# 32 x 32 block transposes on VectorE with transfers in place of TensorE transposes, in four of eight batches, and a later preparation of MLP2's first weights

## The chip, the cores and the metric

The program runs on one core of a Trainium2 chip. The metric is the device time of one execution in microseconds (us), as a median over runs. TensorE (PE in the profile) multiplies matrices, VectorE (DVE), ScalarE (ACT) and GpSimd (POOL) work elementwise, and SyncE (SP) issues nearly all DMA transfers, in order, on one queue.

## The reference

Eight batches go through a cross attention between 512 tokens and 32 state rows per head (8 heads of 64), a first MLP with a softmax-like gate and a normalisation, and a second MLP. Cut to what matters:

```python
# attention, per batch and head: x is 512 x 64, state is 32 x 64
a     = softmax(scale * x @ state.T);  xread = a @ state
a2    = softmax(scale * state @ x.T);  sread = a2 @ x
x = concat(xread, sread)                     # 8 batches of 544 rows of 512
# MLP1 (w_in 512 x 1024, w_out 1024 x 512)
h = x @ w_in
solu = h * softmax(h)
ln = (solu - mean) / sqrt(var + 1e-6) * g_ln
x = ln @ w_out
# MLP2 (w_in 512 x 2048, w_out 2048 x 512)
h = x @ w_in
out = (h * sigmoid(1.702 * h)) @ w_out
```

## The kernel before

Every product of MLP1 and MLP2 is computed from a high and a low part of each factor: three matmuls (high by high, low by high, high by low) for one product, so each factor must first be split in two by ScalarE and VectorE or GpSimd.

The work is described as steps (an engine or a choice of engines, an estimated cost, tiles that are read and written, and a due time), and a planner (`Plan`) puts all steps of the program in one order before the program is built. Each engine then runs its steps strictly in that order. Due times such as 205 are in the planner's own time, which is not the time of the trace. Tiles lie in numbered slots of SBUF: `NSLOT` slots of 2 KB per partition for most tiles (kind "s"), `NRAW` slots for weights as they come from memory (kind "r"), `NWIDE` for the 1024 columns wide tiles of MLP1 (kind "d"). When the last tile of kind "d" is done, that memory becomes further "s" slots for MLP2 (`pl.more`).

The batches overlap. While batch b is in MLP1's first product (`mlp1`, four tiles of 128 tokens, whose product needs two PSUM banks each), batch b-1 is in the second (`mlp1_out`, eight blocks k of 128 inner columns), and batch b+1 is in attention. In `attention`, `x_T(j)` transposes the x of two heads: TensorE makes four 128 x 128 transposes into a PSUM bank, and ScalarE or VectorE copies the bank out. In MLP1, `z_T(b, k)` does the same with the four normalised tiles u of a batch: four 128 x 128 transposes on TensorE, then ScalarE multiplies by g and writes the high part (`zhi`), and VectorE writes the low part (`zlo`), both from PSUM. `mlp1_out(b, k)` then needs both parts. `store_x2` copies the finished batch out of PSUM and stores it (`scr`).

MLP2's weights are 64-bit floats in memory. `to_f32` turns a block of them into 32-bit ones (two passes of ScalarE, three of VectorE, one of GpSimd). MLP2 multiplies in a form with seven instead of eight block products, so the blocks are also added to one another (`sums`, four passes of VectorE) and split. `prepare_up(k, q)` does this for a quarter of the first weight matrix (four blocks, seven results) and stores the results in DRAM (`kept3`); `load_up(j)` reads a part j of four back before the products of step (batch, j) start. Parts j = 0, 1 come from the quarters with q = 0, parts j = 2, 3 from those with q = 1. MLP2 runs over steps in the order (0,0), (1,0), (0,1), (1,1), (0,2), ... of seven products each (`up`), and later over the second weight matrix (`down`).

Of the kernel before, what the change touches and what calls it, by code (L numbers as in the profile page):

```python
# [8 lines left out]
F32 = mybir.dt.float32  # L9
F32R = mybir.dt.float32r  # L10
# [4 lines left out]
AF = mybir.ActivationFunctionType  # L15
ALU = mybir.AluOpType
AX = mybir.AxisListType

NSLOT = 79
NWIDE = 7  # L20
NRAW = 2
AHEAD = 30.092
KF = 11.222
LOOK = 27.436
# [8 lines left out]
LEAD = 62.849  # L33
KEEP = 5
PP = 1.33
FIRST = "d"


class Tl:
# [301 lines left out]
def attention_solu_gelu(ctx: ExitStack, tc: tile.TileContext, x, state, w1, w2, g_ln, w3, w4, out):  # L341
# [28 lines left out]
    pl.kind("s", slot_p, NSLOT)  # L370
    pl.kind("d", first_p, NWIDE)
    pl.kind("r", slot_p, NRAW)
    pl.first, pl.late = first_p, None
    pl.kind("t", slot_p, 4)
    pl.kind("y", slot_p, 28)
# [8 lines left out]
    def ACT(c):  # L384
        return [("act", c)]

    def DVE(c):
        return [("dve", c)]
# [7 lines left out]
    def DMA(c=0.55):  # L396
        return [("dma", c)]
# [102 lines left out]
    def attention(b):  # L500
# [14 lines left out]
        for j in range(1, NP):  # L515
            load_x(b, j)

        def x_T(j):
            p = tl("m", [P, 512], F32, f"pxT{b}_{j}")
            xt[j] = tl("s", [P, S], F32, f"xT{b}_{j}")  # L520

            def go(e):
                for c in range(C):
                    e.transpose(p()[:, c * P:(c + 1) * P], xn[b, j]()[:, c].rearrange("p a d -> p (a d)"), ident)

            do(PE(.44), go, [xn[b, j]], [p], key())
            do([("act", .48), ("dve", .6)], lambda e: copy(e, xt[j](), p()), [p], [xt[j]])
# [199 lines left out]
    def mlp1(b, i, key):  # L727
# [21 lines left out]
        def hf():  # L749
# [17 lines left out]
        do([("dve", .72), ("pool", 1.2)], lambda e: e.tensor_scalar(u(), u(), s()[:, 3:4], s()[:, 7:8], op0=ALU.add, op1=ALU.mult),  # L767
           [s, u], [u])
        return mm

    def z_T(b, k, key):
        n = n_tiles[b] * P
# [71 lines left out]
    def prepare_up(k, q, due):  # L844

        blocks = [to_f32(rows(w3, k + 2 * j, q + 2 * i), f"w3_{k}{q}{i}{j}", due - 3, keep=KEEP)
                  for i in range(2) for j in range(2)]
        for i, t in enumerate(sums("a", blocks, f"w3_{k}{q}")):
            for h, t in zip("hl", split(t, f"w3s{i}_{k}{q}", due)):
                o = kept3[i, q, h]  # L850
                do(DMA(), lambda e, o=o, t=t: e.dma_start(out=o()[:, k], in_=t().bitcast(F32)), [t], [o], key=due + 5,
                   nbytes=P * 2048, join=began3.get((i, q, h)))
                began3.setdefault((i, q, h), pl.steps[-1])

    def load_up(j, due, after):

        q, c = divmod(j, 2)
        for i in range(7):
            w = W3[i, j] = [tl("s", [P, 2, 256], F32R, f"w3r{i}_{j}{h}") for h in "hl"]
            for h, t in zip("hl", w):  # L860
                o = kept3[i, q, h]
                do(DMA(), lambda e, o=o, t=t, c=c: e.dma_start(out=t().bitcast(F32), in_=o()[:, :, 256 * c:256 * c + 256]),
                   [o], [t], key=due, after=after, keep=RK, nbytes=P * 2048)
# [254 lines left out]
             for i in range(7) for q in range(2) for h in "hl"}  # L1118
    began3 = {}
    for n, (q, k) in enumerate((q, k) for q in range(2) for k in range(2)):  # L1120
        prepare_up(k, q, SLOT + (n + 1) * (base2 - 40 - SLOT) / 4)
    attention(0)
    for b in range(B):
        if b + 1 == DIRECT:
# [14 lines left out]
    for b in range(B + 1):  # L1139
        acc = [tl("w", [P, 2, 512], F32, f"accA{b}_{a}") for a in range(2)]  # L1140
        base = (b + 1) * SLOT if b < B else B * SLOT + 27
        per = SLOT / K1 if b < B - 1 else (3.3 if b < B else 1.7)
        if b == 0:
            base, per = M2A, M2S
        for k in range(K1):
            z_T(b, k, base + k * per - ZL)
            mlp1_out(b, k, acc, base + k * per)
        store_x2(b, acc, base + K1 * per + 2)
    per = 7 * PP
# [4 lines left out]
        at[c, j] = base  # L1154
        base += per if c < B else 4 * PP
    base3 = base + 3 * PP
    for j in range(NM // 2):
        load_up(j, at[0, j] - 6, [last[B]])
    x2, kept4 = {}, {}
    for n, (c, j) in enumerate(steps):  # L1160
# [17 lines left out]
            base += per  # L1178
        finish(c, acc, base)
    down_plain(base)  # L1180
    pl.more(2 * NWIDE)
    pl.plan()
    pl.emit()

# [25 lines left out]
```

## Time and profile before

| | |
|---|---|
| median of 3 runs | 1157.05 us (1156.01 to 1157.98) |
| the profiled execution | 1153.79 us, of which the span of instructions is 1152.0 us |
| TensorE busy | 1103.9 us, 96% of the span |
| VectorE busy | 798.0 us, 69% |
| ScalarE, GpSimd busy | 643.4 us, 254.9 us |
| mean granted TensorE clock | 0.988 |

Busy times overlap between engines. TensorE's matmuls are pipelined and their recorded durations overlap one another, so a matmul's price is the distance from one start to the next. An engine's idle time only costs something where the work that ends last waits for it; a share of the whole span hides stretches in which another engine is the full one.

### The profile page before, as it was taken

Reading aid. Unit: us, or ns where it says so; the run is one execution under the profiler, and the core shown is the slowest. Engines: PE = TensorE matmul, PEld = TensorE weight load, DVE = VectorE, ACT = ScalarE, POOL = GpSimd, SP = SyncE. Lnnn points to the kernel's source line nnn. Section 1 sums busy time; section 2 is a strip of 40 time slices with the busy share of each in tenths; the row PEclk is TensorE's granted clock in tenths of the full one; section 3 lists DMA queues with packets and bytes.
Section 4 is the critical chain, followed back from the end, with each engine's and each line's share of the span. In section 5 each row is a group of like instructions: output and inputs, shape, how many; then the busy total and the mean of one; then the engine's idle time right before and its main releaser. Section 6 shows DMA issues by size and latency. Waiting matters only on the chain.

```text
span 1152.0 us, 21763 instructions
## 1 busy us (share of the span) xinstructions
PE 1103.9 (96%) x8239; PEld 1000.0 (87%) x8239; DVE 798.0 (69%) x1336; ACT 643.4 (56%) x1187; POOL 254.9 (22%) x218
## 2 busy tenths in 40 slices
PE   5889889989999989999999999999999999999998
PEld 2567667767777868999999999999999999999998
DVE  6999895695886754427567656715578897788780
ACT  6687765975785645447566656645344443344440
POOL 3865582553575430001011001000000000000000
PEclk8899999999999999999999999999999999999999
DMA  8214253063140449757677576649963254344411
GB/s 244 58 55 129 72 171 110 26 205 105 37 183 2 155 165 344 267 184 266 220 247 251 207 241 208 229 147 397 379 212 94 91 164 141 104 142 147 166 59 52
DMA packets 148600, 192.27 MB, mean 167 GB/s; under 512 B 44304, under 2 KB 90384, under 8 KB 148496
## 3 DMA queue, kind: packets, MB, share of 16 engines
q1 hardware_dynamic: 148400, 190.76, 49.9%
q8 instruction: 64, 1.05, 0.4%
q14 instruction: 40, 0.33, 0.1%
q10 hardware_dynamic: 96, 0.13, 0.0%
HBM read 108.01 MB, written 82.84 MB: 166 GB/s over the span
## 4 chain that ended last, share of the span: by engine, by line
PE 77%; DVE 16%; ACT 3%; issue 2%; DMA 1%; POOL 0%; SPq 0%; DVEq 0%; ACTq 0%; POOLq 0%
PE psum L961 9%; PE psum L960 9%; PE psum L962 9%; PE psum L1039 9%; PE psum L1040 9%; PE psum L1041 9%; PE psum L418 5%; PE psum L420 5%; PE psum L419 5%; DVE w_w L445 2%; DVE w_w L440 2%; DVE u L756 2%; DVE w_w L443 1%; ACT v L459 1%; DVE zlo L785 1%
## 5 line engine op out<-in xcount | busy, mean ns | idle before, releaser
L1039 PE MATMUL psum<-w4r,hi_g 128*128 128x256 f32 x896 | 251.6, 281 | 1.6 <-DVE oc L1050 1.6
L1040 PE MATMUL psum<-w4r,hi_g 128*128 128x256 f32 x896 | 251.5, 281 | 0.0
L1041 PE MATMUL psum<-w4r,lo_g 128*128 128x256 f32 x896 | 251.5, 281 | 0.0
L1039 PEld LDWEIGHTS psum<-w4r,hi_g 128*128 128x128 f32 x896 | 169.1, 189 | 1.8 <-ACT hi_g L459 1.8
L1041 PEld LDWEIGHTS psum<-w4r,lo_g 128*128 128x128 f32 x896 | 169.0, 189 | 0.0
L1040 PEld LDWEIGHTS psum<-w4r,hi_g 128*128 128x128 f32 x896 | 168.9, 189 | 0.0
L459 ACT CAST hi_g<-a_g 128x512 fp32r<-128x512 f32 x124 | 75.1, 620 | 120.6 <-DVE a_g L830 86.3
L447 POOL TENSOR_TENSOR w_w<-w_w,raw_w 128x512 uint32<-128x512 uint32 x48 | 66.6, 1395 | 290.3 <-DVE w_w L445 209.5
L972 DVE TENSOR_TENSOR c<-psum,u 128x512 f32<-128x512 f32 x64 | 44.1, 690 | 107.8 <-PE psum L962 68.8
L418 PE MATMUL psum<-zhi,hi_w 128*128 128x512 f32 (+1 forms) x288 | 115.9, 402 | 1.7 <-DVE u L756 1.1
L419 PE MATMUL psum<-zlo,hi_w 128*128 128x512 f32 (+1 forms) x288 | 110.3, 383 | 0.1
L420 PE MATMUL psum<-zhi,lo_w 128*128 128x512 f32 (+1 forms) x288 | 110.2, 383 | 0.0
L907 DVE TENSOR_TENSOR lo_g<-a_g,hi_g 128x512 fp32r<-128x512 f32 x128 | 83.8, 685 | 18.9 <-PE psum L1040 7.3
L944 ACT ACTIVATE t<-c 128x512 f32<-128x512 f32 x96 | 60.6, 632 | 47.8 <-DVE c L972 47.2
L907 DVE TENSOR_TENSOR lo_g<-gr,hi_g 128x512 fp32r<-128x512 f32 x104 | 70.9, 685 | 10.7 <-ACT hi_g L459 9.2
L459 ACT CAST hi_g<-gr 128x512 fp32r<-128x512 f32 x104 | 61.4, 618 | 28.1 <-PE psum L1040 15.3
L783 ACT ACTIVATE zhi<-psum,g_sb 128x512 fp32r<-128x512 f32 (+1 forms) x72 | 46.9, 664 | 41.7 <-PE psum L777 34.8
L418 PEld LDWEIGHTS psum<-zhi,hi_w 128*128 128x128 f32 x288 | 54.5, 189 | 15.1 <-issue 4.1
L785 DVE SCALAR_TENSOR_TENSOR zlo<-psum,g_sb,zhi 128x512 fp32r<-128x512 f32 (+1 forms) x72 | 51.0, 715 | 22.1 <-ACT zhi L783 20.8
L420 PEld LDWEIGHTS psum<-zhi,lo_w 128*128 128x128 f32 x288 | 54.4, 189 | 11.4
L961 PE MATMUL psum<-lo_x,w3r_3h 128*128 128x256 f32 x224 | 63.0, 281 | 0.0
L962 PE MATMUL psum<-hi_x,w3r_3l 128*128 128x256 f32 x224 | 63.0, 281 | 0.0
(249 smaller groups left out, 3134.9 us busy)
## 6 DMA issues: line engine op xcount, KB each, us to landing
g<-t SPq DMA_DIRECT2D x136, 256.0 KB, 2.3
gr<-g SPq DMA_DIRECT2D x136, 256.0 KB, 3.7
w4r<-w4k SPq DMA_DIRECT2D x56, 256.0 KB, 5.2
raw_w<-in_moe_w_in SPq DMA_DIRECT2D x24, 512.0 KB, 4.8
raw_w<-in_moe_w_out SPq DMA_DIRECT2D x24, 512.0 KB, 4.9
xb<-scr SPq DMA_DIRECT2D x34, 256.0 KB, 6.0
scr<-x SPq DMA_DIRECT2D x16, 512.0 KB, 3.2
out<-oc SPq DMA_DIRECT2D x32, 256.0 KB, 3.1
```

The source lines that it names most:

```text
L418: nc.tensor.matmul(o, lhi, rhi, start=first, stop=False)
L419: nc.tensor.matmul(o, lhi, rlo, start=False, stop=False)
L420: nc.tensor.matmul(o, llo, rhi, start=False, stop=last)
L447: do(POOL(1.23), lambda e: e.tensor_tensor(u(), u(), raw()[:, :, 0], op=ALU.add), [w, raw], [w], key=due)
L459: e.copy(o, i)
L907: do(DVE(.68), lambda e: e.tensor_tensor(flat_(lo), flat_(t), flat_(hi), op=ALU.subtract), [t, hi], [lo], key=due)
L960: nc.tensor.matmul(o, wh()[:, k, cut], hi()[:, k, :], start=first and not mi + k, stop=False, **OPEN)
L961: nc.tensor.matmul(o, wh()[:, k, cut], lo()[:, k, :], start=False, stop=False, **OPEN)
L962: nc.tensor.matmul(o, wl()[:, k, cut], hi()[:, k, :], start=False, stop=bool(mi and k), **OPEN)
L1039: nc.tensor.matmul(o, hi()[:, mi, cut], wt[:, 0], start=first, stop=False, **OPEN)
L1040: nc.tensor.matmul(o, hi()[:, mi, cut], wt[:, 1], start=False, stop=False, **OPEN)
L1041: nc.tensor.matmul(o, lo()[:, mi, cut], wt[:, 0], start=False, stop=2 * j + mi == NM - 1 and u == 1, **OPEN)
```

## The change

Three things change. First, for batches 4 to 7 the x of two heads is no longer transposed by TensorE. Four transfers bring x from memory so that 32 x 32 blocks already lie where they belong, and one VectorE pass transposes each block in place (`x_T_dma`). The untransposed x is still loaded as well. Second, for the same batches `z_T` runs only for k = 0 to 3. The other half is made by `z_turn`: four VectorE passes transpose the 32 x 32 blocks of the four u tiles into a wide tile, sixteen transfers move the blocks from SBUF to SBUF to their places, and then ScalarE and VectorE make the high and the low part for k = 4 to 7, now from SBUF instead of PSUM. Two wide tiles each for the two sides (kind "z", `NZ`) take the place of eight "s" slots. Third, the four calls of `prepare_up` had due times 111.4, 182.4, 253.3 and 324.3 in the planner's time; now three have 205, 255 and 310, and the fourth comes after MLP2's first step has been planned, 16 before step (0,2).

```diff
-NSLOT = 79
+NSLOT = 71
+NZ = 2
+ZB = 4
+XD = 4
-FIRST = "d"
+FIRST = "dz"
...
+        def x_T_dma(j):
+            t = tl("s", [P, C, S // (C * 32), 32], F32, f"xb{b}_{j}")
+            xt[j] = tl("s", [P, S], F32, f"xT{b}_{j}")
+            first = None
+            for q in range(4):
+                src = x[b, 2 * j + q // 2].rearrange("(r t c) d -> t c r d", t=32, c=C)[:, :, :, 32 * (q % 2):32 * (q % 2) + 32]
+                s = do(DMA(.65), lambda e, q=q, src=src: e.dma_start(out=t()[32 * q:32 * q + 32], in_=src), writes=[t],
+                       nbytes=P * 1024, join=first)
+                first = first or s
+            key()
+            do(DVE(.6), lambda e: e.transpose(out=xt[j](), in_=t().rearrange("p c r f -> p (c r f)")), [t], [xt[j]])
+
         def x_T(j):
+            if b >= XD:
+                return x_T_dma(j)
...
+    def z_turn(b, half, due):
+        w = tl("z", [P, C, 512], F32, f"zw{b}_{half}")
+        z = tl("z", [P, C, 512], F32R, f"z{b}_{half}")
+        for i in range(C):
+            t = w.part(lambda ap, i=i: ap[:, i, :])
+            do(DVE(.6), lambda e, t=t, i=i: e.transpose(out=t(), in_=u_t[b, i]()[:, 512 * half:512 * half + 512]),
+               [u_t[b, i]], [t])
...
+        for q0 in range(4):
+            for r in range(4):
+                def go(e, r=r, q=(q0 + r) % 4):
+                    src = w()[32 * r:32 * r + 32].rearrange("f i (k q t) -> f i k q t", q=4, t=32)[:, :, :, q, :]
+                    dst = z()[32 * q:32 * q + 32].rearrange("f i (k r t) -> f i k r t", r=4, t=32)[:, :, :, r, :]
...
+                s = do(DMA(.65), go, [w], [z], key=due - 3, nbytes=P * 1024, join=first)
...
+        for j in range(4):
+            k = 4 * half + j
+            hi = tl("s", [P, C, P], F32R, f"zhi{b}_{k}")
+            lo = z.part(lambda ap, j=j: ap[:, :, j * P:(j + 1) * P])
+            do(ACT(.57), lambda e, hi=hi, lo=lo, k=k: e.activation(hi(), lo().bitcast(F32), AF.Identity,
+                                                                  scale=g_sb[:, k:k + 1]), [lo, g_t], [hi])
+            do(DVE(.67), lambda e, hi=hi, lo=lo, k=k: e.scalar_tensor_tensor(
+                out=lo(), in0=lo().bitcast(F32), scalar=g_sb[:, k:k + 1], in1=hi(), op0=ALU.mult, op1=ALU.subtract),
+               [lo, hi, g_t], [lo])
+            z_t[b, k] = (hi, lo)
...
-        prepare_up(k, q, SLOT + (n + 1) * (base2 - 40 - SLOT) / 4)
+        if n < 3:
+            prepare_up(k, q, (205, 255, 310)[n])
...
+        if ZB <= b < B:
+            z_turn(b, 1, base + 4 * per - ZL)
         for k in range(K1):
-            z_T(b, k, base + k * per - ZL)
+            if (b, k) not in z_t:
+                z_T(b, k, base + k * per - ZL)
...
-    for j in range(NM // 2):
+    for j in range(NM // 4):
+        load_up(j, at[0, j] - 6, [last[B]])
+    prepare_up(1, 1, at[0, 2] - 16)
+    for j in range(NM // 4, NM // 2):
         load_up(j, at[0, j] - 6, [last[B]])
...
-    pl.more(2 * NWIDE)
+    pl.more(2 * NWIDE + 4 * NZ)
```

The planner makes a new order of this. Three places of it follow, in the form "line, operation, written tile <- read tiles, shape"; names begin with the tile's name in the program, with the batch in it.

The first place is VectorE where the second product of batch 3 ends and that of batch 4 begins. `zlo3_7` is the last low part of batch 3, `sml` and `u` are the statistics and tiles of `mlp1`. Before:

```order
L785 SCALAR_TENSOR_TENSOR zlo3_7_2917<-psum_69,g_sb_81,zhi3_7_2908 128x512
L761 TENSOR_SCALAR sml4_3_2869<-sml4_3_2869 128x1
L764 TENSOR_SCALAR sml4_3_2869<-sml4_3_2869 128x1
L752 TENSOR_REDUCE sml5_0_2939<-psum_69 128x1
L756 SCALAR_TENSOR_TENSOR u5_0_2957,sml5_0_2939<-psum_69,u5_0_2957 128x1024
L785 SCALAR_TENSOR_TENSOR zlo4_0_2985<-psum_69,g_sb_81,zhi4_0_2968 128x512
```

The same place now:

```order
L533 STREAM_TRANSPOSE xT6_0_2756<-xb6_0_2654 128x512
L533 STREAM_TRANSPOSE xT6_1_2763<-xb6_1_2685 128x512
L797 STREAM_TRANSPOSE zw4_1_2771<-u4_0_2411 128x512
L775 SCALAR_TENSOR_TENSOR u4_3_2761,sml4_3_2724<-psum_69,u4_3_2761 128x1024
L835 SCALAR_TENSOR_TENSOR zlo3_7_2791<-psum_69,g_sb_81,zhi3_7_2774 128x512
L780 TENSOR_SCALAR sml4_3_2724<-sml4_3_2724 128x1
L880 TENSOR_TENSOR a1_w3_00_2803<-w_w3_0010_2695,w_w3_0011_2706 128x512
L465 CAST hi_w3s4_00_2812<-a1_w3_00_2803 128x512
L797 STREAM_TRANSPOSE zw4_1_2771<-u4_1_2461 128x512
L783 TENSOR_SCALAR sml4_3_2724<-sml4_3_2724 128x1
L797 STREAM_TRANSPOSE zw4_1_2771<-u4_2_2561 128x512
```

Between the same steps of MLP1 there now stand transposes of x and of u, and passes of the first weight preparation (`w3_00`), which stood earlier before.

The second place is SyncE's queue where batch 6 leaves MLP1. `scr6` is the store of batch 6, `w3r` are loads of MLP2's prepared weights. Before:

```order
L807 DMA scr6_101<-x2_6_0_4306 128x1024
L807 DMA scr6_101<-x2_6_1_4323 128x1024
L862 DMA w3r0_0h_4357<-w3k0_0h_104 128x2x256
L862 DMA w3r0_0l_4362<-w3k0_0l_105 128x2x256
L862 DMA w3r1_0h_4367<-w3k1_0h_108 128x2x256
```

The same place now, with all sixteen transfers of batch 7's `z_turn` in one row:

```order
L857 DMA scr6_101<-x2_6_0_4247 128x1024
L806 DMA z7_1_4282<-zw7_1_4043 32x16x32 x16
L857 DMA scr6_101<-x2_6_1_4284 128x1024
L912 DMA w3r0_0h_4371<-w3k0_0h_104 128x2x256
L912 DMA w3r0_0l_4376<-w3k0_0l_105 128x2x256
L912 DMA w3r1_0h_4381<-w3k1_0h_108 128x2x256
```

The sixteen transfers stand behind the first store of batch 6 and ahead of its second store and of all weight loads.

The third place is VectorE in MLP2's first four steps. `c11`, `c12` and `c22` (batch and step behind) are the sums that each step makes of its products. Before, they follow one another:

```order
L972 TENSOR_TENSOR c11_1_0_4970<-psum_69,x1_1_0_4954 128x512
L972 TENSOR_TENSOR c12_0_0_5021<-psum_69,u1_0_0_4885 128x512
L972 TENSOR_TENSOR c22_1_0_5040<-psum_69,u2_1_0_5037 128x512
L972 TENSOR_TENSOR c11_0_1_5071<-psum_69,x1_0_1_5054 128x512
L972 TENSOR_TENSOR c12_1_0_5117<-psum_69,u1_1_0_5005 128x512
```

Now the second half of the fourth preparation (`w3_11`, its last two blocks 1100 and 1101) stands between them:

```order
L1022 TENSOR_TENSOR c12_0_0_4933<-psum_69,u1_0_0_4790 128x512
L444 TENSOR_SCALAR w_w3_1100_4949<-w_w3_1100_4949 128x512
L447 TENSOR_SCALAR w_w3_1100_4949<-w_w3_1100_4949 128x512
L449 SCALAR_TENSOR_TENSOR w_w3_1100_4949<-raw_w3_1100_4831,w_w3_1100_4949 128x512
L1022 TENSOR_TENSOR c22_1_0_4976<-psum_69,u2_1_0_4971 128x512
L444 TENSOR_SCALAR w_w3_1101_4974<-w_w3_1101_4974 128x512
L447 TENSOR_SCALAR w_w3_1101_4974<-w_w3_1101_4974 128x512
L449 SCALAR_TENSOR_TENSOR w_w3_1101_4974<-raw_w3_1101_4854,w_w3_1101_4974 128x512
L880 TENSOR_TENSOR a2_w3_11_5018<-a1_w3_11_4870,w_w3_1100_4949 128x512
L880 TENSOR_TENSOR a3_w3_11_5022<-w_w3_1110_4671,w_w3_1100_4949 128x512
L1022 TENSOR_TENSOR c11_0_1_5040<-psum_69,x1_0_1_4993 128x512
L880 TENSOR_TENSOR a4_w3_11_5049<-w_w3_1101_4974,a2_w3_11_5018 128x512
```

The last sum, `a4`, now stands behind `c11` of step (0,1) in VectorE's order, and step (0,2) needs what is made of it.

## Rows read from the trace of the kernel before

**Rows 1.** The page: busy time, share and instructions of each engine.

```profile
PE 1103.9 (96%) x8239; PEld 1000.0 (87%) x8239; DVE 798.0 (69%) x1336; ACT 643.4 (56%) x1187; POOL 254.9 (22%) x218
```

**Rows 2.** Windows by stage: length, busy PE, PEld, DVE, ACT, POOL, PEclk, DMA.

```profile
130.00:257.00 127.00, 118.22 (x684) 90.02 (x682) 101.88 (x172) 91.80 (x179) 70.00 (x56) 0.99 0.38 122
257.00:403.00 146.00, 142.34 (x860) 111.01 (x859) 107.99 (x193) 97.66 (x194) 73.75 (x66) 1.00 0.29 96
403.00:466.00 63.00, 57.90 (x317) 48.93 (x316) 33.93 (x55) 28.67 (x50) 11.06 (x10) 0.97 0.80 263
466.00:503.00 37.00, 37.00 (x316) 37.00 (x315) 11.13 (x17) 17.47 (x30) 0.00 (x0) 1.00 0.68 235
```

**Rows 3.** Waits of TensorE, 130 to 466: us in total, times, longest.

```profile
PE psum L418 <- DVE u L756: 10.8, 6, 5.1
```

**Rows 4.** Windows where VectorE is full, where it isn't, and behind two waits.

```profile
130.00:170.00 40.00, 36.18 (x234) 27.66 (x232) 39.30 (x65) 28.12 (x60) 29.30 (x23) 0.99 0.47 147
180.00:230.00 50.00, 48.60 (x293) 37.16 (x292) 31.73 (x62) 37.48 (x73) 20.28 (x19) 1.00 0.23 66
340.00:400.00 60.00, 60.00 (x342) 47.99 (x340) 41.67 (x77) 36.09 (x73) 28.14 (x27) 1.00 0.21 75
170.00:180.00 10.00, 9.67 (x44) 7.84 (x45) 4.14 (x8) 5.64 (x9) 3.12 (x4) 0.86 0.15 57
410.00:420.00 10.00, 8.37 (x31) 6.71 (x32) 3.45 (x7) 1.74 (x3) 1.74 (x2) 0.83 0.28 105
```

**Rows 5.** TensorE in order of time around two groups of transposes.

```profile
291.77 0.40 PE L420 MATMUL psum<-zhi,lo_w 128*128 128x512 f32 x1
292.00 0.60 PE L524 MATMUL psum<-ident,xn 128*128 128x128 f32 x4
292.44 0.60 PE L777 MATMUL psum<-ident,u 128*128 128x128 f32 x4
...
293.11 0.39 PE L419 MATMUL psum<-lo_v,ahi 128*128 128x512 f32 x1
```

**Rows 6.** Groups of VectorE by line and shape, 0 to 420: busy, mean ns.

```profile
L785 DVE SCALAR_TENSOR_TENSOR zlo<-psum,g_sb,zhi 128x512 fp32r<-128x512 f32 x56 | 41.1, 743 | 7.3 <-ACT zhi L783 6.2 <-POOL lo_w3s L454 1.0
...
L445 DVE SCALAR_TENSOR_TENSOR w_w<-raw_w,w_w 128x512 uint32<-128x512 uint32 x32 | 28.2, 898 | 0.4
L440 DVE TENSOR_SCALAR w_w<-w_w 128x512 f32<-128x512 f32 x32 | 25.1, 794 | 3.7 <-ACT w_w L439 3.6
L443 DVE TENSOR_SCALAR w_w<-w_w 128x512 uint32<-128x512 uint32 x32 | 20.4, 647 | 0.6
...
L587 DVE STREAM_TRANSPOSE aT<-s 128x512 f32<-128x512 f32 x16 | 11.1, 699 | 2.0 <-POOL s L584 2.0
...
L830 DVE TENSOR_TENSOR a_w<-w_w,w_w 128x512 f32<-128x512 f32 x8 | 10.0, 1250 | 1.0 <-POOL w_w L447 1.0
```

**Rows 7.** VectorE in order of time from 405.91: start, duration.

```profile
405.91 1.79 DVE L830 TENSOR_TENSOR a_w<-w_w,w_w 128x512 f32<-128x512 f32 x1
...
409.74 0.69 DVE L454 TENSOR_TENSOR lo_w3s<-a_w,hi_w3s 128x512 fp32r<-128x512 f32 x1
410.35 1.22 DVE L756 SCALAR_TENSOR_TENSOR u<-psum,u 128x1024 f32<-128x1024 f32 x1
```

**Rows 8.** Transfers: count, size each, median us to landing.

```profile
raw_w<-in_moe_w_out SPq DMA_DIRECT2D x24, 512.0 KB, 4.9
...
xn<-in_x SPq DMA_DIRECT2D x56, 128.0 KB, 3.4
...
w3r_2h<-w3k_1h SPq DMA_DIRECT2D x7, 256.0 KB, 5.6
```

**Rows 9.** The tile xn: issue times of its transfers in ns, minimum, median, maximum.

```profile
L476 SPq DMA_DIRECT2D xn<-in_x x56: 539/621/3642, 9.3 to 289.0; - x56
```

**Rows 10.** The tiles w3r_0h and w3r_2h: durations, first and last start.

```profile
L960 PE MATMUL psum<-hi_x,w3r_0h x224: 274/281/287, 466.0 to 759.0; 128*128 128x256 f32 x112
...
L960 PE MATMUL psum<-hi_x,w3r_2h x224: 274/281/290, 502.8 to 790.2; 128*128 128x256 f32 x112
```

More of the change, by code (lines that the diff above doesn't have):

```diff
@@ L372, in attention_solu_gelu @@
     pl.kind("r", slot_p, NRAW)
+    pl.kind("z", first_p, NZ)
     pl.first, pl.late = first_p, None
@@ L769, in mlp1 @@
         return mm
+    def z_turn(b, half, due):
[5 more added lines that the diff above has]
+               [u_t[b, i]], [t])
+            w.wrote += t.wrote
+        first = None
+        for q0 in range(4):
[3 more added lines that the diff above has]
+                    dst = z()[32 * q:32 * q + 32].rearrange("f i (k r t) -> f i k r t", r=4, t=32)[:, :, :, r, :]
+                    e.dma_start(out=dst.rearrange("f i k t -> f (i k) t").bitcast(F32),
+                                in_=src.rearrange("f i k t -> f (i k) t"))
+                s = do(DMA(.65), go, [w], [z], key=due - 3, nbytes=P * 1024, join=first)
+                first = first or s
+        for j in range(4):
[8 more added lines that the diff above has]
+            z_t[b, k] = (hi, lo)
     def z_T(b, k, key):
```

## The prediction

> **What bounds the kernel now.** The page says TensorE, 96% busy [rows 1]. That share hides where the other 48 us lie, so I read windows by stage next [rows 2]. From 466 on (MLP2) TensorE is busy all the time. From 130 to 466, where batches 1 to 8 go through MLP1 beside attention, it is busy 8.8 us less than the first window's length, 3.7 less than the second's and 5.1 less than the third's: 17.5 us. The waits name VectorE: 10.8 us for `u` of line 756, which frees the PSUM banks of an `mlp1` tile, the longest 5.1 [rows 3]. Cutting finer shows why. Where VectorE is full (39.3 of 40 us), TensorE gets 36.2 of 40, about 90%; where VectorE is at 63 to 69%, TensorE gets 48.6 of 50 and 60 of 60 [rows 4]. The full places are the weight preparations: the 5.1 us wait ends with a `u` that stands in VectorE's queue behind sums of 1.79 us each [rows 7]. Two waits also cost clock: the mean of the 10 us around or behind them is 0.86 and 0.83 of full speed [rows 4], so TensorE runs at the lower of its two levels, 1.2 GHz, for part of each and loses 1.4 and 1.7 us more. So the limit is TensorE with VectorE close behind it, and each piece of work that leaves one for the other must be counted on both.
>
> **TensorE's part.** A group of four transposes: the L419 at 293.11 would follow the L420 at 291.77 by two steps of 0.23 (292.00 - 291.77); it comes 1.34 behind, and two groups lie between, so (1.34 - 0.46) / 2 = 0.44 us each [rows 5]. Sixteen groups of x and sixteen of z go: 14.1 us. In the new order eight of them leave the stretch that was 130 to 257, twenty the one from 257 to 403, four the last; three `mlp1` parts of 6 matmuls (1.4 us each) move from the last stretch into the second.
>
> **VectorE's part**, counted in the new order against the old. A block's conversion is three passes of 0.79, 0.65 and 0.90, mean 0.78; a sum is 1.25; a 32 x 32 transpose pass is 0.70; a low part 0.74 [rows 6].
> - First stretch: 23 conversion passes (-17.9), 8 sums (-10.0) and 7 splits (about -7) leave; 8 transposes of x come (+5.6) and 11 small passes shift in (about +7). 101.9 falls to about 80.
> - Second stretch: 12 conversion passes (+9.4), 4 sums (+5.0), 8 transposes of x and 15 of z (+16.1) and 5 small copies (+1) come, 4 passes go (-2). Twelve low parts now read two tiles from SBUF instead of one and PSUM. Such passes last 0.69 when GpSimd has nothing to do and up to 1.79 beside it [rows 7]; the nearest in form, L445, has a mean of 0.90 [rows 6]. Between 0.69 and 1.79 I take 1.1, so +0.36 each (+4.3), and one more of them (+1). Neighbouring passes overlap by some 0.08 us in the record, so of 41 added passes 3.3 comes off: 108.0 + 31.5 = about 139, between 135 and 151.
>
> The Trainium skill's rule speaks against this part: its page GPSIMD Engine Reference, section Specifications, says that GpSimd's SBUF interfaces are shared with VectorE and collide when VectorE has two SBUF inputs. By that rule the moved low parts are the ones to suffer, and [rows 7] agree: 1.79 and 0.69 us for the same shape. If all twelve paid the full 1.79, the stretch would have 147 instead of 139.
>
> **The sum by stretches**, against the profiled execution (1153.8 us, 3.3 below the median; I subtract from the median).
> - *Ahead of 130*: the order is the same but for a few passes. 0.
> - *130 to 257 (127 us)*: TensorE 118.2 - 8 x 0.44 - 1.4 (the clock of one wait) = 113.3. VectorE at 80 of some 115 is like the uncrowded windows, where TensorE loses 0 to 3%. I take 2 us: 115.3, so -11.7 (bounds -13.7 and -7).
> - *257 to 403 (146 us)*: TensorE 142.3 - 8.8 + 4.2 = 137.7. VectorE now needs 139: it is full throughout. It can't be under 141 (139 / 0.983). At the 90% of the full windows TensorE would take 153; with all low parts dear, 157. I take 148, nearer to the middle since here the extra work is spread and not in one burst: +2 (bounds -5 and +11).
> - *403 to 466 (63 us)*: TensorE 57.9 - 1.8 - 4.2 - 1.7 = 50.2. The preparation that caused the 5.1 us wait is not here any more. New is a wait for batch 7's second half of z. Its 16 transfers stand in SyncE's queue behind the first store of batch 6. Nearest row for the issue of such a transfer, 512 pieces each: 0.62, with 3.4 to land [rows 8, 9]. 16 x 0.62 + 3.4, then 0.7 on ScalarE and 0.9 on VectorE, is 14.9; about 3.5 us go ahead of it for the copy, its queue on ScalarE and the store. TensorE has 78 matmuls of 0.23 and 1.7 us of transposes in between, 19.7. The margin is about 1 us. Bounds: issue at 0.54 (no wait) and at 0.9 (4 us). I take 2: 52.2, so -10.8 (bounds -12.8 and -7).
> - *MLP2's start*: step (0,2) begins 36.8 us behind the first product, 502.8 against 466.0 [rows 10], with TensorE busy in all of it [rows 2]. The fourth preparation must be through by then. Only two raw slots exist, so blocks 1100 and 1101 are fetched when GpSimd has finished the first two, by my count 8 us after the first product (VectorE is busy with x's factors until about 6). Then 4.9 to land, 1.4 on ScalarE, 2.3 on VectorE and about 1.4 on GpSimd for the first block, 2 more for the second: 20. Two sums 2.5, three low parts in a row on GpSimd about 5: 27.5. Storing 2.5, the fifth load issued 2.5 later, 5.6 to land: 38. So 0 to 6 us late; the stores and sums have slack that I can't see. I take 1.5.
>
> -11.7 + 2 - 10.8 + 1.5 = -19.0: **1138 us**. The bounds together would be 1125 and 1160. The rest of MLP2 is costed at nothing: its products are unchanged and VectorE has 11 of 37 us in use there [rows 2].
>
> **The rivals.**
> - *VectorE takes it back* (A). For it: full VectorE costs TensorE 10% everywhere it is seen. Against it: no burst as dense as the old preparations. All low parts and sums at the dear price, second stretch 157, and batch 7's z 3 us later: 1147 to 1154. 15%.
> - *The transfers are slow* (B), the one that ends on the other side. The z pieces are 128 bytes; the smallest transfers in rows 8 are of 256-byte pieces. If each of the sixteen takes t instead of 0.62, batch 7 is late by 16 (t - 0.62) - 1, and batches 4 to 6, with some 5 us to spare, by 16 (t - 0.62) - 5 each. The four waits eat the 19 us when t reaches 1.18; at twice 0.62 the result is 1161 to 1168 with the clock lost in the waits. 11%. The Trainium skill's page DMA: Bandwidth & Descriptors, section Specifications, says that below 512 bytes a piece the engines read, modify and write and don't reach line rate. By that rule this rival would be nearer than I hold it; the trace has 256-byte pieces landing at 3.4 us per 128 KB [rows 8], which is no such collapse, and none of 128.
> - *The fourth preparation is late* (C): 7 to 10 us at step (0,2), for the chain above has no slack: 1144 to 1148. 7%.
> - *Better than taken* (D): VectorE keeps pace, second stretch 141, no wait for z or the weights: 1127, from 1120 to 1131. 12%.
>
> **How the numbers follow.** Likeliest, 48%: 1131 to 1147 around 1138. A 15, C 7, D 12, together with it 82% faster by over 0.2% (2.3 us, about what a measurement of this kernel can tell from no change). 7% within 0.2%, where A, C and the wait for z come together. 11% slower (B). To leave out no more than 2 in 10, the range reaches from 1126 into D's lower part to 1157, past A.
>
> **What would show it.** Right: in the new profile TensorE's transposes of x and those of z have 64 matmuls fewer each; the first preparation no longer stands before the middle of batch 3; TensorE's idle time from batch 1 to batch 3 is about 2 us; VectorE is 95% or more busy over the second stretch and TensorE idle there for some 10 us, on VectorE's `u` or low parts; the first product of MLP2 comes about 20 us earlier. Wrong: VectorE's new low parts at 1.5 us or more (A); z's transfers at 1 us or more each, and TensorE waiting for the z parts at k = 4 of each batch (B); TensorE idle for over 5 us ahead of the third weight part (C). A gain made in MLP2, behind its step (0,2), would be none of my steps.

## The result, and the profile after

The change takes the kernel from 1156.01 us (1155.09 to 1157.98, median of 5 runs on the same chip) to 1138.19 us (1135.91 to 1140.18): a ratio of 0.9843, with a 95% interval from 0.9828 to 0.9859. The profiled execution took 1138.69 us, with a span of 1136.9. The predicted time was 1138 us. The sum came out, but not each of its terms, and the reason given for one of them did not hold as it stood.

The page after, engines first, to be read against [rows 1]:

```profile
span 1136.9 us, 21706 instructions
PE 1091.8 (96%) x8111; PEld 987.6 (87%) x8111; DVE 811.9 (71%) x1370; ACT 636.8 (56%) x1168; POOL 257.7 (23%) x219
```

TensorE has 128 matmuls less (8239 before), which are the 32 groups of four transposes. VectorE has 13.9 us more. Whole-span shares say nothing of where that went, so here are the windows by stage, cut at the same products as [rows 2] (batch 1's first, batch 3's fifth, batch 6's seventh, and MLP2's first): length, busy time of PE, PEld, DVE, ACT and POOL, granted clock, share of the DMA engines, GB/s.

```profile
131.00:243.00 112.00, 111.29 (x645) 84.86 (x644) 77.93 (x150) 70.39 (x138) 39.92 (x39) 1.00 0.29 68
243.00:399.00 156.00, 144.65 (x805) 109.74 (x804) 139.37 (x240) 109.95 (x211) 97.20 (x80) 0.97 0.64 173
399.00:449.00 50.00, 50.00 (x282) 42.96 (x281) 24.41 (x44) 25.05 (x44) 4.31 (x6) 1.00 0.70 210
449.00:490.00 41.00, 39.83 (x335) 39.41 (x334) 27.58 (x38) 25.68 (x45) 15.57 (x9) 1.00 1.00 346
```

The three stretches to MLP2 are now 112.7, 155.8 and 49.7 us long by the starts of those products (126.7, 146.5 and 62.8 before). The first and the third have almost no idle TensorE left. The second has 11.35 us of it where it had 3.66, and a mean clock of 0.97 where it had 1.00. Its waits, the longest of TensorE between 243 and 399 (us in total, times, longest), are spread over many tiles:

```profile
PE psum L423 <- DVE z L816: 2.2, 1, 2.2
PE psum L648 <- DVE sr L641: 2.0, 1, 2.0
PE psum L422 <- DVE u L775: 1.4, 3, 1.0
PE psum L621 <- ACT e2t L583: 1.1, 1, 1.1
PE psum L827 <- ACT stT L463: 1.1, 1, 1.1
```

The clock fell three times there, each time within a microsecond of the end of such waits (at 272.93 and 274.59, at 309.06 and at 390.74). The windows of 10 us around the three places, in the same columns as above:

```profile
270.00:280.00 10.00, 7.85 (x29) 5.12 (x27) 8.41 (x11) 4.47 (x9) 3.53 (x4) 0.83 0.87 286
310.00:320.00 10.00, 10.00 (x42) 7.99 (x41) 7.23 (x15) 4.69 (x8) 4.95 (x5) 0.86 0.18 60
390.00:400.00 10.00, 9.26 (x33) 7.44 (x34) 8.73 (x14) 4.44 (x8) 7.76 (x8) 0.83 0.57 211
```

They lose 1.7 + 1.4 + 1.7 us, and about 0.3 more on the other side of 310, in all 5.1 us, for TensorE runs at the lower of its levels, 1.2 GHz, for part of each. Before the change there was none in this stretch, and one each in the first and in the third [rows 4].

The new work on VectorE (busy us, mean ns; 243 to 449), and the new transfers (count, KB each, median us to landing):

```profile
L816 DVE SCALAR_TENSOR_TENSOR z<-z,g_sb,zhi 128x512 fp32r<-128x512 f32 x16 | 14.0, 898 | 5.2 <-ACT zhi L814 5.2
L797 DVE STREAM_TRANSPOSE zw<-u 128x512 f32<-128x512 f32 x16 | 11.2, 700 | 3.3 <-POOL u L786 3.2 <-DVE zlo L835 0.2
...
L533 DVE STREAM_TRANSPOSE xT<-xb 128x512 f32<-128x512 f32 x8 | 5.4, 690 | 0.8 <-PE psum L424 0.8
```

```profile
xb<-in_x SPq DMA_DIRECT2D x64, 64.0 KB, 2.5
z<-zw SPq DMA_DIRECT2D x64, 64.0 KB, 2.3
```

The transposes cost 0.70 us each, as on [rows 6]. The moved low parts have a mean of 0.90, where the prediction took 1.1.

### The profile page after: what moved, and what is told of

Same layout as the page of the kernel before. It is cut to its first block, busy times and chain, and to the rows that moved or that the text cites. A ratio compares the mean times of both kernels' runs of the same rounds, so it can differ in the third digit from the quotient of the medians.

```text
span 1136.9 us, 21706 instructions
## 1 busy us (share of the span) xinstructions
PE 1091.8 (96%) x8111; PEld 987.6 (87%) x8111; DVE 811.9 (71%) x1370; ACT 636.8 (56%) x1168; POOL 257.7 (23%) x219
## 4 chain that ended last, share of the span: by engine, by line
PE 57%; DVE 1%; DMA 1%; POOL 0%; issue 0%; ACT 0%; POOLq 0%; DVEq 0%; ACTq 0%
PE psum L1089 9%; PE psum L1090 9%; PE psum L1091 9%; PE psum L1010 9%; PE psum L1011 9%; PE psum L1012 9%; PE psum L1137 1%; PE psum L1057 1%; PE psum L1136 1%; PE psum L1058 1%; PE psum L1056 1%; PE psum L1135 1%; DMA w3k_1l<-lo_w3s 0%; DVE lo_x L957 0%; DMA w3k_1h<-hi_w3s 0%
## 5 line engine op out<-in xcount | busy, mean ns | idle before, releaser
L423 PE MATMUL psum<-zlo,hi_w 128*128 128x512 f32 (+1 forms) x224 | 85.7, 382 | 0.1
L424 PEld LDWEIGHTS psum<-zhi,lo_w 128*128 128x128 f32 x288 | 55.5, 193 | 11.6
L1010 PE MATMUL psum<-hi_x,w3r_1h 128*128 128x256 f32 x224 | 63.0, 281 | 1.2 <-ACT u L1017 1.2
L1011 PE MATMUL psum<-lo_x,w3r_2h 128*128 128x256 f32 x224 | 63.0, 281 | 0.0
L1011 PE MATMUL psum<-lo_x,w3r_0h 128*128 128x256 f32 x224 | 63.0, 281 | 0.0
```

What stands on the lines that cost most here:

```text
L423: nc.tensor.matmul(o, lhi, rlo, start=False, stop=False)
L424: nc.tensor.matmul(o, llo, rhi, start=False, stop=last)
L1010: nc.tensor.matmul(o, wh()[:, k, cut], hi()[:, k, :], start=first and not mi + k, stop=False, **OPEN)
L1011: nc.tensor.matmul(o, wh()[:, k, cut], lo()[:, k, :], start=False, stop=False, **OPEN)
```

## The experiments

The theory ahead of the runs was the prediction's: TensorE is the limit with VectorE close behind it; the transposes give TensorE 14 us, the preparations' stalls go from the first and third stretch, and a full VectorE gives some of it back in the second. The rivals were that only one of the two edits makes the gain, that the transfers set the pace, and that the order of single steps does. The diffs are against the changed kernel. All times are medians; each ratio is to the kernel before, measured beside it on the same chip, with its 95% interval.

| kernel | us | ratio to before |
|---|---|---|
| the change | 1138.19 | 0.9843 (0.9828 to 0.9859) |
| preparations moved, no transposes (e1) | 1149.36 | 0.9952 (0.9937 to 0.9967) |
| transposes, preparations not moved (e2) | 1135.25 | 0.9830 (0.9811 to 0.9850) |
| moved, x alone (e3) | 1142.28 | 0.9897 (0.9880 to 0.9915) |
| moved, z alone (e4) | 1146.42 | 0.9927 (0.9913 to 0.9942) |
| not moved, x alone (e11) | 1150.70 | 0.9948 (0.9930 to 0.9966) |
| the change, due times one later (e5) | 1138.91 | 0.9859 (0.9842 to 0.9875) |
| the change, z in 32 transfers (e6) | 1175.31 | 1.0172 (1.0157 to 1.0187) |
| the change, one preparation left out (e9) | 1135.09 | 0.9829 (0.9811 to 0.9846) |
| the change, one of three left in the loop (e14) | 1137.17 | 0.9833 (0.9816 to 0.9849) |
| e2, x of batches 2 and 3 too (e10) | 1139.25 | 0.9859 (0.9844 to 0.9874) |
| e2, other due times (e13) | 1144.30 | 0.9892 (0.9876 to 0.9908) |
| e2, preparations spread (e12) | 1137.79 | 0.9838 (0.9823 to 0.9853) |

**The two edits apart.** e1 has the new due times and the old transposes:

```
-NSLOT = 71
+NSLOT = 79
...
-ZB = 4
-XD = 4
+ZB = 8
+XD = 8
...
```

> The preparations stand where the change puts them; all transposes of x and z are TensorE's again, as in the kernel before (and the memory slots as before). Theory (TensorE is the limit with VectorE close behind; both parts give, each on its own): the 32 groups of 0.44 us come back, 14.1 us on TensorE, but VectorE in the second stretch falls from 139 to about 118 us of work and its share of TensorE's 11 us of idle time there goes with it, some 5 us: 1138 + 14 - 5 = 1147, from 1143 to 1151. First rival (the move of the preparations makes the gain, the transposes only shift work between two nearly full engines): 1138 within 3. Second rival (the transposes make it, the move only makes room on VectorE): 1153 to 1157.

It took 1149.36, inside the theory's range. `ZB` and `XD` are the first batches whose z and x leave TensorE; with 8 none does. e2 has the new transposes and the old due times:

```
-        if n < 3:
-            prepare_up(k, q, (205, 255, 310)[n])
+        prepare_up(k, q, SLOT + (n + 1) * (base2 - 40 - SLOT) / 4)
...
-    prepare_up(1, 1, at[0, 2] - 16)
```

> x and z are transposed as in the change, the four preparations have the due times of the kernel before. Theory: TensorE's 14.1 us go, but the first stretch keeps its dense preparations (VectorE 102 + 5.6 us), and the second gets 24 us more on VectorE beside one and a half preparations, 108 + 23 = 131 of about 140; the third keeps its wait of 5 us behind the sums. So -3 in the first stretch, -5 in the second, -2 in the third, 1156 - 10 = 1146, from 1142 to 1151. First rival (the move makes the gain): 1153 or more. Second rival (the transposes make it): 1138 to 1141.

It took 1135.25, and here the theory failed by 11 us: the transposes alone give all that the change gives. Moving the preparations gives 5.6 us when it stands alone and nothing that can be measured on top of the transposes (0.9843 and 0.9830, with intervals that overlap). The windows say why. First those of e2, then those of e1, in the columns from above:

```profile
131.00:252.00 121.00, 113.90 (x649) 86.83 (x648) 100.32 (x175) 83.62 (x161) 55.94 (x49) 0.97 0.44 122
252.00:397.00 145.00, 138.75 (x806) 106.68 (x805) 124.21 (x229) 101.43 (x197) 83.95 (x72) 1.00 0.57 145
397.00:449.00 52.00, 50.48 (x279) 42.66 (x278) 30.09 (x48) 27.03 (x47) 12.16 (x10) 1.00 0.83 259
```

```profile
131.00:247.00 116.00, 115.62 (x683) 89.05 (x682) 77.17 (x149) 74.83 (x147) 43.90 (x42) 1.00 0.19 54
247.00:402.00 155.00, 144.18 (x860) 112.74 (x859) 122.48 (x208) 106.29 (x208) 89.53 (x74) 0.98 0.39 132
402.00:458.00 56.00, 56.00 (x318) 47.82 (x316) 27.20 (x48) 30.29 (x53) 5.27 (x6) 1.00 0.68 225
```

Adding up the three windows of each kernel gives this table, where the clock's loss is read from windows of 10 us, as above (the clock of a long window is rounded too coarsely for it), MLP2 is the span less the start of its first product, and before is from [rows 2, 10]:

| | busy TensorE | of it lost to clock | idle | MLP2 |
|---|---|---|---|---|
| before | 318.5 | 3.4 | 17.5 | 686.0 |
| moved only (e1) | 315.8 | 3.4 | 11.2 | 690.3 |
| transposes only (e2) | 303.1 | 3.4 | 14.9 | 686.3 |
| both (the change) | 305.9 | 5.1 | 12.1 | 688.1 |

Busy time without the clock's part falls by 15.4 us (before to e2) and by 11.6 (e1 to the change) through the transposes, a mean of 13.5. The predicted 32 x 0.44 is 14.1. The move by itself takes 6.3 us of idle time away and puts 4.3 onto MLP2; on top of the transposes it takes 2.8 away and costs 1.8 in MLP2 and 1.7 of clock. It clears the first and the third stretch, and the waits stand in the second instead (10.8 us idle in e1, 11.35 in the change, 6.25 in e2). In e1 nearly all of them are of the kind that [rows 3] show:

```profile
PE psum L421 <- DVE u L774: 9.4, 6, 4.0
```

How the transposes alone can take a wait away is seen in the third stretch. There the prediction held the fourth preparation to be the cause of a wait of 5.1 us, since a `u`, the third from last, stood behind two sums and a row of splits and ran at 410.35 [rows 7]. In e2 the same sums run within 2 us of the same time, but that `u` has run at 388.0, ahead of them. The next one meets them. VectorE of e2 in order of time:

```profile
403.36 1.60 DVE L880 TENSOR_TENSOR a_w<-w_w,a_w 128x512 f32<-128x512 f32 x1
404.88 0.68 DVE L880 TENSOR_TENSOR a_w<-w_w,w_w 128x512 f32<-128x512 f32 x1
405.49 1.40 DVE L835 SCALAR_TENSOR_TENSOR zlo<-psum,g_sb,zhi 128x512 fp32r<-128x512 f32 x2
406.81 1.21 DVE L775 SCALAR_TENSOR_TENSOR u<-psum,u 128x1024 f32<-128x1024 f32 x1
...
407.94 1.78 DVE L458 TENSOR_TENSOR lo_w3s<-a_w,hi_w3s 128x512 fp32r<-128x512 f32 x1
```

It stands ahead of the splits. TensorE waits 1.5 us in the whole stretch, 0.5 of it for `u`. So the wait went by a changed order, with the preparation still in its place.

**x and z apart.** e3 sets `ZB = 8`, e4 sets `XD = 8`, both with the new due times; e11 is e3 with the old ones (each with the memory slots that belong to it).

> New preparations, x of batches 4 to 7 by transfers and one VectorE pass, z on TensorE as before. Theory: 16 groups of z come back to TensorE, 7.0 us, of which 12 groups (5.3 us) in the second stretch and 4 in the third; VectorE there loses 16 transposes of 0.70 and reads its low parts from PSUM again (0.74 in place of about 1.1): 139 - 10 - 5 = 124, so TensorE's idle time there falls by some 4: 1138 + 7 - 4 = 1141, from 1138 to 1145. If z's transfers cost time that can't be seen (they bring the wait for z back), this kernel would be faster than the change, 1135 or less.

> New preparations, half of z of batches 4 to 7 by VectorE and transfers, all of x on TensorE as before. Theory: 16 groups of x come back, 7.0 us, 8 of them in the first stretch (3.5 us, full price, as VectorE has room there) and 8 in the second, where VectorE loses 8 passes of 0.70 but its copies of the transposed x out of PSUM may come back to it or to ScalarE: 1138 + 3.5 + 2 = 1143.5, from 1140 to 1147. If the extra 128-byte transfers of x disturbed others, this kernel would be at 1138 or below.

> The kernel before with nothing but x of batches 4 to 7 transferred and transposed by VectorE; z on TensorE, preparations and memory slots as before. With the kernel that has both transposes and the old due times (1135.25) it splits that gain in x's part and z's. TensorE loses 16 groups of 0.44, 7.0 us. Theory (each half gives what TensorE saves): 1156 - 7 = 1149, from 1146 to 1151, and z's half the remaining 14. Rival (x's half brings most of it): 1143 or less. Rival (only both together shift the order of the last batches past the preparation at 400 us): 1152 or more.

All three came out within the theory's ranges (1142.28, 1146.42, 1150.70). In busy time less the clock's part, e11 is at 306.6 us against 315.1 before, so 16 groups of x are worth 8.5, and the 16 of z that e2 has on top 6.8. The rest of z's 13.6 us between e11 and e2 (0.0118 of 1156) is mostly idle time and clock: e11 still has the old third stretch, 62.8 us long, and e2 has 51.9.

**Is it a full VectorE that costs in the second stretch?** e9 leaves the second preparation out, e14 the second and the third of the three that stand there; the results of one that is kept are stored a second time in the place of those that are missing (the diff is e14's):

```
-                do(DMA(), lambda e, o=o, t=t: e.dma_start(out=o()[:, k], in_=t().bitcast(F32)), [t], [o], key=due + 5,
+                for m in range(2):
+                    do(DMA(), lambda e, o=o, t=t, m=m: e.dma_start(out=o()[:, m], in_=t().bitcast(F32)), [t], [o], key=due + 5,
...
-        if n < 3:
+        if n < 1:
```

> The changed kernel without its second preparation (k = 1, q = 0; the parts of the first are stored a second time in its place, so the weights of that quarter are copies of another's). It runs at 323 to 345 us in the trace of the changed kernel, where the kernel waits 2.0 us at 309, 1.4 at 342 and 0.7 at 357 and loses 1.7 us of clock behind the first. Theory (what the second stretch costs are the stalls at the preparations, about 4 to 6 us each, wherever they stand): 5 us less, 1133, from 1130 to 1135; TensorE's idle time from batch 3 to batch 6 falls from 11.3 to about 7. Rival (VectorE is full with the transposes and low parts, and the preparation only fills gaps): 1136 or more. Rival (transfers of z on SyncE's queue set the pace): no change, 1138.

> The changed kernel with one preparation in place of three between batch 3 and batch 6, and the late one at MLP2's start as it is (each of the two is stored twice, so half of MLP2's first weights are copies of the others). VectorE in the second stretch falls from 139 us to some 95. If it was the full VectorE that cost TensorE there: idle time falls from 11.3 to about 4 and two of three falls of the clock go: 1138 - 11 = 1127, from 1123 to 1131. Rival (the waits come from the chain of attention, transposes and z itself and only change their place, as leaving out one preparation suggests, with 10.9 of 11.3 us of idle time still there): 1132 to 1136.

e9 gave 1135.09, at the edge of what the theory allowed. Its second stretch is 3.9 us shorter, 3.4 of that through the clock; idle time did not fall as expected (10.88 us in the stretch, not 7). e14 gave 1137.17, no gain that can be measured, where the theory said 1127. Its second stretch is 5.6 us shorter (150.2), 3.4 of that through the clock, and MLP2 takes 5.0 longer, with 2.6 us of waiting for a part of the weights; the doubled stores of the late preparation, which no other kernel has, are the likely cause, which was not tested. VectorE is 77% busy in the stretch in place of 89%, and TensorE is still idle for 9.44 us.

That looks like the end of the theory, but the sum over the stretch hides where the idle time lies. The preparation that e14 keeps runs between 250 and 276; the two that it leaves out run between 312 and 396 in the changed kernel. Here are the second stretches cut in two at 316. First the front part, of the change and of e14, then the rest, of the change (two preparations), e9 (one) and e14 (none):

```profile
243.00:316.00 73.00, 66.85 (x409) 50.58 (x408) 66.44 (x121) 52.68 (x104) 44.12 (x38) 0.95 0.68 167
244.00:316.00 72.00, 63.35 (x398) 46.53 (x396) 62.67 (x108) 52.24 (x106) 43.74 (x37) 0.99 0.73 195
```

```profile
316.00:399.00 83.00, 77.81 (x398) 59.17 (x397) 72.92 (x120) 57.28 (x108) 53.08 (x42) 0.98 0.60 178
316.00:394.00 78.00, 75.93 (x403) 59.31 (x402) 63.44 (x106) 49.85 (x95) 44.01 (x37) 1.00 0.51 139
316.00:394.00 78.00, 77.21 (x406) 60.84 (x405) 52.80 (x92) 41.73 (x80) 25.02 (x24) 0.99 0.31 65
```

Behind 316 TensorE is idle for 5.2, 2.1 and 0.8 us, with VectorE at 88, 81 and 68%: there the two preparations do cost idle time, as the theory said, some 4 us between them. In front of it e14 is idle for 8.65 us where the change is for 6.15. That part still has its preparation and VectorE at 87 to 91%, and e14's doubled stores stand in SyncE's queue ahead of batch 4's z, whose first transfer is issued at 282.77 in place of 275.23. So neither run tells what the front part would cost without a preparation.

Single waits show how a preparation reaches TensorE. The longest of the changed kernel's second stretch, first TensorE's row and then VectorE's in order of time:

```profile
390.74 0.50 PE L423 MATMUL psum<-z,hi_w 128*128 128x512 f32 x1 [2.23 <-DVE z L816]
```

```profile
387.12 1.27 DVE L449 SCALAR_TENSOR_TENSOR w_w<-raw_w,w_w 128x512 uint32<-128x512 uint32 x1
388.31 0.68 DVE L880 TENSOR_TENSOR a_w<-a_w,w_w 128x512 f32<-128x512 f32 x1
388.92 1.77 DVE L816 SCALAR_TENSOR_TENSOR z<-z,g_sb,zhi 128x512 fp32r<-128x512 f32 x1
```

The low part of z stands behind a conversion pass and a sum of the third preparation; its high part has been ready since 385.97, so the transfers were in time. A wait that is put down to ScalarE can be of the same kind. e14's longest, 2.2 us, is for the copy `stT`, which stands behind a copy that itself waited for a sum of the kept preparation on VectorE:

```profile
273.20 0.62 ACT L463 CAST hi_w3s<-a_w 128x512 fp32r<-128x512 f32 x1 [1.05 <-DVE a_w L880]
273.73 0.68 ACT L833 ACTIVATE zhi<-psum,g_sb 128x512 fp32r<-128x512 f32 x1
274.31 0.36 ACT L463 COPY stT<-psum 128x256 f32<-128x256 f32 x1
```

**The transfers.** e6 issues each of z's sixteen transfers as two halves:

```
-                    e.dma_start(out=dst.rearrange("f i k t -> f (i k) t").bitcast(F32),
-                                in_=src.rearrange("f i k t -> f (i k) t"))
+                    for i in (0, 2):
+                        e.dma_start(out=dst[:, i:i + 2].rearrange("f i k t -> f (i k) t").bitcast(F32),
+                                    in_=src[:, i:i + 2].rearrange("f i k t -> f (i k) t"))
```

> Each of the sixteen transfers of a z is issued as two of half the size, in the same place; nothing else moves. SyncE's queue has 16 x 0.6 = 10 us more to issue ahead of each of the four z. Theory (z comes early enough in three batches out of four; only batch 6's low part made TensorE wait, 2.2 us): 10 us more make three or four waits of 3 to 8 us where the margin is 2 to 7: 1138 + 10 = 1148, from 1141 to 1158. Rival (z has much room): within 2 of 1138. Rival (the transfers already set the pace of the second stretch): 1138 + 4 x 10 = 1175 or more.

It took 1175.31, as the last rival said: 37 us more for some 38 us of issue (128 transfers at a median of 0.61 us in place of 64 at 0.63). In SyncE's queue the first z took 12.12 us in the changed kernel and takes 21.67 here (first row the change, second e6):

```profile
275.23 12.12 SPq L806 DMA_DIRECT2D z<-zw  x16
```

```profile
276.22 21.67 SPq L807 DMA_DIRECT2D z<-zw  x32
```

TensorE's longest waits of e6 between 243 and 470, and ScalarE in order of time before two of them:

```profile
PE psum L422 <- ACT zhi L815: 11.9, 2, 9.0
PE psum L621 <- ACT e2t L583: 10.6, 1, 10.6
PE psum L422 <- ACT v L463: 8.3, 1, 8.3
```

```profile
299.59 1.33 ACT L815 ACTIVATE zhi<-z,g_sb 128x512 fp32r<-128x512 f32 x2 [7.98 <-DMA z<-zw]
300.83 2.35 ACT L463 COPY v<-psum 64x512 f32<-64x512 f32 x4
...
353.06 0.66 ACT L443 ACTIVATE w_w<-raw_w 128x512 f32<-128x512 f32 x1 [9.99 <-DMA w3k_0h<-hi_w3s]
```

Two kinds of queue hold things up. At 299.59 ScalarE, which works strictly in order, stands at z's high part, and the copies `v` behind it, which TensorE needs, have nothing to do with z. At 353.06 ScalarE waits for room that a store of prepared weights must free, and that store stands in SyncE's queue behind the second z's transfers. In the changed kernel the same wait is 0.46 us long:

```profile
336.40 0.67 ACT L443 ACTIVATE w_w<-raw_w 128x512 f32<-128x512 f32 x1 [0.46 <-DMA w3k_0h<-hi_w3s]
```

So the changed kernel has little room left. TensorE's idle time from 244 to MLP2 rises by 30.5 us, 7.6 a batch, for some 9.4 of issue added to each, so some 2 us a batch were to spare (an estimate, and from this one size of delay); the rest of the 37 us is mostly a lower clock (0.91 and 0.92 in the last two stretches).

**Order, place and spread.** e5 sets the due times to 206, 256 and 311. e10 sets `XD = 2` in e2. e13 gives e2 the due times 145, 200, 255 and 324.3. e12 sets a block's due time to `due - 3 - 6 * (3 - 2 * i - j)` and a split's to `due + 3 * (i - 3)` in e2.

> The changed kernel with the three due times of the preparations one unit later (206, 256, 311). It does the same work; the planner makes a slightly other order. It measures how far an order alone moves the time. Theory: within 2 of 1138. If the order of single steps decides where stalls fall, 3 to 6 us to either side, and differences of that size between the other kernels have to be read with care.

> The transposes of the change and the due times of the kernel before for all four preparations (1135.25 on the chip so far), with x of batches 2 and 3 transferred and transposed by VectorE as well: 8 groups of 0.44 us less on TensorE, 8 passes of 0.70 more on VectorE, in and ahead of the first stretch, where VectorE has 100 of 121 us in use. Theory: TensorE's 3.5 us come out, and about 1 goes to stalls at the first preparation: 1133, from 1131 to 1135. Rival (VectorE there is as good as full): 1135 to 1139.

> Both transposes as in the change; the preparations due at 145, 200, 255 and 324.3, so that the first leaves the place where it stalls TensorE by 6.6 us and the clock falls (160 to 178 us with the old due times), and the fourth stays ahead of MLP2. If a preparation's stall depends on what VectorE does beside it, the emptier place of the first (VectorE 64 to 82% between 180 and 230) should take it for 2 us in place of 10: 1135.25 - 8 = 1128, from 1125 to 1131. Rival (a preparation costs about the same wherever it stands): 1133 to 1138.

> Both transposes as in the change, due times of the kernel before, but the four blocks of a preparation are due 6 apart and the splits 3 apart, so that one preparation is spread over some 35 us and not 20. If the density of the burst makes the stalls: the idle time from 130 us to MLP2, 14.9 us with the old due times, and two falls of the clock (5 us) shrink by half: 1135.25 - 8 = 1127, from 1123 to 1131. Rival (the amount of work counts): 1133 to 1138.

e5's 1138.91 shows that an order changed a little moves nothing that can be measured. e10 missed: 1139.25, no faster than e2. Of its 32 removed matmuls 26 stand ahead of 131 us (595 there in place of 621), where TensorE is idle for over 25 us anyway: its busy time there falls from 105.51 to 103.86 us, the mean clock from 0.90 to 0.86, and the stretch ends only 0.8 us sooner. e13 missed too, at 1144.30. The first stretch did become shorter, 115.9 us in place of 120.7, with 3.2 us idle in place of 7.1. But the second and third preparation had been moved along with it, and in the second stretch idle time rose from 6.25 to 12.07 us. So it does not answer its own question cleanly; it shows that the places count, by 7 to 9 us. e12 is as e2 within the intervals: spreading the preparations took away the fall of the clock that e2 has between 130 us and MLP2 (3.4 us), and idle time rose from 14.9 to 17.2 us. No version beat the change by more than the intervals allow.

## Why the prediction was right, point by point

- **TensorE's 14.1 us: right.** The two comparisons give 15.4 and 11.6, a mean of 13.5, and x's half (8.5) and z's half (6.8) lie on either side of the 7.0 that was reckoned for each. The price of a group, read from the distance of two matmuls [rows 5], held.
- **First stretch, -11.7: it was -14.0.** VectorE fell to 78 us (80 predicted) and TensorE's idle time to 0.7 (2 taken). Here the reason held: with the preparation back in the stretch, e2 needs 120.7 us and has 7.1 of idle time.
- **Second stretch, +2: it was +9.3, and this is the step that failed.** VectorE's 139 us came out at 139.4, TensorE's idle 10 at 11.35. The rest did not. The prediction took no fall of the clock there, and three cost 5.1 us; 1.7 more are TensorE's own work, 139.4 us (155.8 less 11.35 and 5.1) in place of 137.7. The reason, "VectorE now needs 139: it is full throughout", was wrong as put: VectorE is 89% busy there, not the 95% or more that was to show it. It is full in places, and these places cost: behind 316 TensorE's idle time went from 5.2 us to 0.8 with the two preparations there. The prediction placed its 148 between 141 and 157 "since here the extra work is spread and not in one burst". That the idle time came out near the 10 in it is partly luck, since it was a choice between two bounds and was not worked out from waits.
- **Third stretch, -10.8: it was -13.1.** The 2 us for batch 7's z did not come; TensorE has no idle time between 399 and 449. The transfers were issued from 411.14 to 421.84, and the low part began at 424.65:

```profile
411.14 10.70 SPq L806 DMA_DIRECT2D z<-zw  x16
```

```profile
424.65 2.08 DVE L816 SCALAR_TENSOR_TENSOR z<-z,g_sb,zhi 128x512 fp32r<-128x512 f32 x3 [5.18 <-ACT zhi L814]
```

  TensorE's first matmul with it starts at 425.69, right in order. The other part of this term, that the 5.1 us wait goes because the preparation goes, isn't needed: e2 keeps the preparation there and waits 1.5.
- **MLP2's start, +1.5: MLP2 as a whole took 2.1 longer.** At its start TensorE waits for 1.2 us in two pieces, but for a copy of ScalarE that frees a PSUM bank (`u` of line 1017), and not for the weights, so rival C did not happen. ScalarE has 25.7 us of work in those 41, where it had 17.5 in 37 [rows 2].
- **Ahead of 130: 0, it was +0.6.**
- **Rival A** did not happen: the low parts have a mean of 0.90. The Trainium skill's page GPSIMD Engine Reference, section Specifications, names collisions between GpSimd and VectorE when VectorE has two SBUF inputs. The trace agrees for single passes only: the seven that ran while GpSimd was idle took 0.74 or 0.75 us, and of the nine beside a working GpSimd six took 0.66 to 0.75 and three 1.31, 1.77 and 1.78.
- **Rival B** was nearer than its 11%. Its spare time of "some 5 us" for batches 4 to 6 was some 2 by the estimate from e6. With 38 us of issue added, 37 are lost; in proportion, which no second size of delay tests, the transfers would have eaten the 19 us at 0.62 + 19 / 64 = 0.92 us each, not 1.18; they took a mean of 0.69. It was kept off by the issue time read from [rows 9], which held for pieces of 128 bytes. The Trainium skill's page DMA: Bandwidth & Descriptors, section Specifications, names 512 bytes as the least piece for full rate; no run here shows a loss by it, since what cost time was SyncE's issue and not the landing (2.3 us).

The stretches add up to +0.6 - 14.0 + 9.3 - 13.1 + 2.1 = -15.1 us between the two profiled spans; the medians are 17.8 apart, as the profiled execution of before was below its median. So the total was right for one reason that held (TensorE's work) and by luck besides: errors of 7.3 us one way and 4.6 the other cancelled in part. MLP2's first product came 17.2 us earlier (466.0 and 448.8), not the 20 that were to show it.

What stays open is what sets the idle time in the front part of the second stretch, 6 to 9 us between 243 and 316 in the change, e9 and e14. One preparation stands there in all three, VectorE is 86 to 91% busy, and e9 and e14 have the doubled stores as well; a kernel without a preparation there was not run. Nor is it shown why spreading the preparations (e12) did not lower the idle time.

## What to carry to other kernels

When work leaves the engine that is the limit, its own price comes out nearly in full if it stands in a stretch where that engine is busy; the same saving in a stretch where it waits (e10) is worth nothing. Of two edits that remove the same waits only one is paid, so each has to be tried alone before both are kept: here the new due times could go. A mean over a stretch hides places in it, so an experiment that takes work out of a stretch is read place by place: e14's total showed no gain, and the part that had been emptied showed one. And count the transfers that a change puts on one queue, with everything that stands behind them: in the changed kernel z landed in time, but twice the number of transfers made weights, copies and TensorE late, by nearly as much as was added.

## What the runs showed of the hardware

Issuing a z transfer from SyncE took a median of 0.63 us for 64 KB, and 0.61 us for half of it (e6), and they landed 2.3 and 2.0 us later: the number of transfers counted, not their size. The clock does not follow from a wait's length alone: in the changed kernel two waits of 1.1 and 1.0 us close together, one of 2.0 and one of 2.2 were each time followed by a fall to 1.2 GHz that lost 1.7 us, and in e12 waits of 2.5 us (at 155) and 3.1 us (at 173) by none, with a granted clock of 1.00 in all three stretches.
